# Three order edits at the two ends of a fused attention and MLP kernel: token transposes, the queries' PSUM bank, one addition of the drain

## The chip, the cores and the metric

The kernel runs on one core of one Trainium2 chip, in one launch. Its time is device time in microseconds of that core. The kernel before takes 1280.31 us (median of 3 runs, 1280.17 to 1280.67).

The core has engines with a queue of their own each: TensorE (PE in the profile; its weight loads are PEld), VectorE (DVE), ScalarE (ACT), GpSimd (POOL) and SyncE (SP, which here only issues transfers). Each engine executes its queue in order. They meet through semaphores. Matmuls write to PSUM, a memory of eight banks, from which VectorE and ScalarE read.

## The reference

Tokens are layer-normed once. Branch A is attention of 2048 tokens against a cache of 2048 keys and values with 32 heads of 128; branch B is an MLP with two layer norms; the output gates the one with the other.

```python
def _A_ref(x, k_cache, v_cache, wq, wo):
    q = (x @ wq).reshape(B, Sq, H, Dh).transpose(0, 2, 1, 3)
    scores = einsum("bhqd,bhkd->bhqk", q, k_cache) * (Dh ** -0.5)
    p = softmax(scores, axis=-1)
    o = einsum("bhqk,bhkd->bhqd", p, v_cache)
    return o.transpose(0, 2, 1, 3).reshape(B, Sq, H * Dh) @ wo

def _B_ref(x, w1, w2, w3, w4):
    h = gelu(layernorm(x) @ w1)
    hs = shifted(h) @ w2          # each quarter of h moved by 1 or 2 tokens
    x1 = x + hs
    return x1 + gelu(layernorm(x1) @ w3) @ w4

xn = layernorm(x)
s = _A_ref(xn, k_cache, v_cache, wq, wo)
g = silu(_B_ref(xn, w1, w2, w3, w4))
out = x + s * g
```

Everything is bfloat16 in memory, with 2048 tokens of 512 elements; the MLP is 1792 wide.

## The kernel before, in words

**Units and slots.** The attention is cut into 128 units (line 121): a unit is one head and one block of 512 tokens. Units run by groups of 4 heads, in a group by token block, in a block by head. So units 0 to 3 are heads 0 to 3 on tokens 0 to 511, unit 4 is head 0 on tokens 512 to 1023. A unit has 8 slots. In slot `p` of unit `u`, which is step `n = 8u + p` of the loop at line 695, these are written down in order:

- `s_slot`: two matmuls of 128 keys each against the 512 queries `qT` into the PSUM tile `ps_s` (two of them, two banks each), then ScalarE's exponential of both into `pT` (line 194).
- `pv_slot`: the two matmuls of the values for the slot five steps back (`LAG = 5`), into `ps_o`.
- In slots 0 and 1, `q_mm`: the queries of unit `u + 2` (four matmuls, `ps_q`), and in slot 2 their copy to `qT` by `q_copy`: VectorE's (line 180), but ScalarE's (line 178) for the last units, `u > QUIET + 1`, that is units 123 to 127 (`QUIET` is 121).
- In slot 3, `sums`: four narrow matmuls with a vector of ones give the row sums of unit `u - 1` (`ps_sum`); VectorE takes the reciprocal (line 233), a small transfer writes it to DRAM (`dr`, line 235), and in slot 4 a broadcast reads it back for all partitions (`rb`, line 250). In slot 2 of the next unit, `norm` (line 261) multiplies `ps_o` by it.
- In slots 4 to 6, `wo_mm` (`ps_wo`, the output projection of one tile of 128 tokens that is ready) and its addition to `s_acc` on VectorE (line 328).
- VectorE also adds up the exponentials (`acc`, lines 200 to 211), of which `sums` takes the row sums.
- Chunks of the MLP in slots 2, 3, 6 and 7, with their PSUM tile `ps_m`, until unit 120.

**The two shared PSUM banks.** The pool `psX` has one buffer for each of two tags. "xa" holds `ps_q`, `ps_wo` and `ps_sum`; "xm" holds the MLP's `ps_m`, and from unit 121 on also `ps_sum` (line 225). The next tile of a tag can be written only when the last has been read.

**Order.** `pin` keeps each engine's instructions in the order in which they are written down. Loads are put at steps of the loop by `at(n, ...)`, and run at the end of that step (line 759). SyncE's queue holds the K loads (transposing transfers, a quarter of a head's keys each, line 146), the V loads (half a head each, line 156), the token transposes (`ln1_turn`, line 370), `dr` and `rb`.

**The start.** Token tiles of 128 are normalised on VectorE with GpSimd's reciprocal roots (line 354) and then turned into `xnT`, the operand of the queries. Tiles 0 to 3 are turned on TensorE. Tiles 4 to 7 are turned by transfers after steps 5, 12, 13 and 14 (the third number of each triple in `tokens`, line 661). The queries of unit 4 (`HG`) are made in slots 6 and 7 of unit 2, steps 22 and 23, and need tiles 4 to 7. Lines 670 to 673 put the K pieces and V halves of heads 2 and 3 at their steps.

**The end.** `gate_sum` (lines 299 and 301) is put into units 122 and 124 in slot 4, for two of the last token tiles, on VectorE. In the drain (lines 788 to 807) the last four token tiles are scaled from PSUM by `last_scale` (line 305, VectorE) and added to `s_acc` by `last_out` (line 310), which also issues the output transfer (line 311).

Of the kernel before, what the change touches and what calls it, by code (L numbers as in the profile page):

```python
# [10 lines left out]
FP32 = mybir.dt.float32  # L11
# [6 lines left out]
def kernel(  # L18
# [16 lines left out]
    P = nc.NUM_PARTITIONS  # L35
# [15 lines left out]
    HG = 4 if H % 4 == 0 else (2 if H % 2 == 0 else 1)  # L51
# [13 lines left out]
    def pool(name, bufs=1, space=None, **kw):  # L65
        if space is not None:
            kw["space"] = space
        return tc.tile_pool(name=name, bufs=bufs, **kw)
# [35 lines left out]
    psX = ent(pool("psX", 1, PSUM))  # L104
# [8 lines left out]
    def mm(out, lhsT, rhs, start, stop):  # L113
        pin(nc.tensor.matmul(out=out, lhsT=lhsT, rhs=rhs, start=start, stop=stop))  # L114
# [8 lines left out]
    QUIET = NU - 7  # L123
# [3 lines left out]
    kTs, vBs, wqs, wos, oTs, st = {}, {}, {}, {}, {}, {}  # L127
    todo = defaultdict(list)

    def at(n, fn):  # L130
        todo[n].append(fn)
# [9 lines left out]
    def load_k(h, pieces):  # L141
        w = Sk // KSPLIT
        for i in pieces:
            if i == 0:
                kTs[h] = kp.tile([P, Sk], BF16, name="kT")
            pin(nc.sync.dma_start(
                out=kTs[h][:, i * w:(i + 1) * w],
                in_=A_k_cache[0, h, i * w:(i + 1) * w, :], transpose=True))

    def load_v(h, halves):  # L150
        v = A_v_cache[0, h].rearrange("(i p j) d -> p i j d", p=P, j=KJ)
        for i in halves:
            if i == 0:
                vBs[h] = vp.tile([P, KC, Dh], BF16, name="vb")
            ks = slice(i * KSPLIT // 2, (i + 1) * KSPLIT // 2)
            pin(nc.sync.dma_start(
                out=vBs[h].rearrange("p (i j) d -> p i j d", j=KJ)[:, ks], in_=v[:, ks]))
# [9 lines left out]
    def q_mm(u, dcs):  # L167
        g, qt, hh = units[u]
        if dcs[0] == 0:
            st[u] = dict(psq=psX.tile([P, 512], FP32, tag="xm" if u == HG else "xa", name="ps_q"))  # L170
        for dc in dcs:
            mm(st[u]["psq"][:], wqs[g * HG + hh][:, dc, :],
               xnT[:, dc, qt * 512:(qt + 1) * 512], dc == 0, dc == DC - 1)
# [129 lines left out]
    def last_scale(t, ps):  # L303
        gf, xf = tl[t]
        pin(nc.vector.scalar_tensor_tensor(
            out=gf[:], in0=ps, scalar=0.5, in1=gf[:], op0=ALU.mult, op1=ALU.mult))

    def last_out(t, eng):
        gf, xf = tl.pop(t)
        pin(eng.tensor_tensor(out=xf[:], in0=gf[:], in1=s_acc[:, t, :], op=ALU.add))  # L310
        pin(nc.sync.dma_start(out=out2d[t * P:(t + 1) * P, :], in_=xf[:]))
# [57 lines left out]
    def ln1_turn(t):  # L369
        pin(nc.sync.dma_start_transpose(out=xnT[:, :, t * P:(t + 1) * P], in_=xns.pop(t)[:]))  # L370
# [293 lines left out]
    for t, (stats, apply, turn) in enumerate(tokens, 4):  # L664
# [2 lines left out]
        at(stats, lambda t=t: ln1_stats(t))  # L667
        at(apply, lambda t=t: ln1_apply(t))
        at(turn, lambda t=t: ln1_turn(t))
    for n, h, piece in ((2, 2, 2), (4, 2, 3), (12, 3, 0), (15, 3, 1), (17, 3, 2), (20, 3, 3)):  # L670
        at(n, lambda h=h, piece=piece: load_k(h, (piece,)))
    for n, h, half in ((7, 2, 0), (13, 2, 1), (20, 3, 0), (21, 3, 1)):
        at(n, lambda h=h, half=half: load_v(h, (half,)))
    at(28, ph1_load)
    at(64, w2_load)
# [2 lines left out]
    for g in range(NG - 1):  # L678
        b = (g * QT + QT - 1) * HG
        for hh in range(HG):  # L680
            h = (g + 1) * HG + hh
# [13 lines left out]
    for n in range(NS):  # L695
        u, p = divmod(n, SPU)
# [4 lines left out]
        if u == 0 and p in (1, 3, 5):  # L701
            q_mm(1 + p // 2, range(DC))
        if u == 0 and p in (2, 4, 6):
            q_copy(p // 2)
        if u == HG - 2 and p in (6, 7):
            q_mm(HG, (2 * p - 12, 2 * p - 11))
        if u == HG - 2 and p == 7:
            q_copy(HG)
        if p in (0, 1) and HG - 1 <= u < NU - 2:
            q_mm(u + 2, (2 * p, 2 * p + 1))  # L710
# [90 lines left out]
        wo_part(dst[j], GL, ts[j], range(HG), False, True)  # L801
    for j in range(4):
        last_scale(ts[j], dst[j])
        if j < 2:
            last_out(ts[j], nc.gpsimd)
    for j in (2, 3):
        last_out(ts[j], nc.vector)
    ph.close()

# [29 lines left out]
```

## Time and profile before

| what | value |
|---|---|
| median of 3 runs | 1280.31 us |
| the profiled execution | 1279.53 us |
| its span, first to last instruction | 1277.8 us |
| granted TensorE clock | 0.999 of full |
| exponentials (line 194, ScalarE) | 1024 of 1.03 us |
| matmuls of 512 columns (line 114) | 0.38 us each, started 0.216 us apart |
| VectorE, busy from 1206.2 to 1215.4 us (9.2 us) | 8.32 us |
| VectorE, busy from 1215.4 to 1224.2 us (8.8 us) | 6.95 us |
| last addition of the drain ends | 1274.76 us |

A group's line names the line of the code, the engine, the operation, the output and inputs by the program's names, and how often it ran. In a timeline a line has the start in us from the span's start, the time it took (for several merged instructions, from the first start to the last end), and what it is; in brackets stands how long its engine was idle before it, and what ended that. A line of waits has the engine, what waited, what it waited for, and the sum, the count and the longest in us. An SPq line is the issuing of a transfer; its landing comes later, and the DMA view tells how much later.

### The profile page before, as it was taken

The numbers are of one execution on the slowest core, as the hardware profiler recorded it, in microseconds if no ns is written. First come the engines' busy times: TensorE is split into PE (matmuls) and PEld (weight loads), VectorE is DVE, ScalarE is ACT, GpSimd is POOL, SyncE is SP. The second block draws the span as 40 slices with busy tenths as digits, with TensorE's granted clock in tenths as the row PEclk, the third lists the DMA queues.
The fourth block names the chain that finished last, engine by engine and source line by source line (L and its number), as shares of the span: only waits on it lengthen the run. The fifth ranks groups of instructions, "written<-read, shape, count | busy, mean of one in ns | idle before, by whom it ended". The sixth has DMA issues, their size and how long they took to land.

```text
span 1277.8 us, 17233 instructions
## 1 busy us (share of the span) xinstructions
PE 1257.1 (98%) x6195; PEld 612.1 (48%) x6320; DVE 1019.2 (80%) x1407; ACT 1113.0 (87%) x1195; POOL 137.9 (11%) x241
## 2 busy tenths in 40 slices
PE   8999999999999999999999999999999999999998
PEld 5444444444444444444444444444444444444444
DVE  7888889898788877778887778887777888777886
ACT  7899998888999988899988889998888999888883
POOL 4430003323110010000001000000000000000110
PEclk9999999999999999999999999999999999999999
DMA  9644343455532564134443244523435133542532
GB/s 185 133 106 81 59 79 88 108 124 123 115 77 67 100 110 89 42 75 83 89 93 68 58 85 93 96 42 75 96 80 90 34 70 72 91 105 46 140 76 58
DMA packets 172950, 111.79 MB, mean 87 GB/s; under 512 B 124800, under 2 KB 149888, under 8 KB 172864
## 3 DMA queue, kind: packets, MB, share of 16 engines
q1 hardware_dynamic: 163904, 85.51, 34.3%
q0 software_dynamic: 8672, 24.91, 7.9%
q8 instruction: 49, 0.80, 0.3%
q14 instruction: 37, 0.30, 0.1%
q10 hardware_dynamic: 288, 0.26, 0.1%
HBM read 82.58 MB, written 7.60 MB: 71 GB/s over the span
## 4 chain that ended last, share of the span: by engine, by line
PE 87%; ACT 6%; DVE 4%; issue 1%; DMA 1%; POOL 0%; DVEq 0%; ACTq 0%
PE ps_s L114 31%; PE ps_o L114 30%; PE ps_m L114 9%; PE ps_wo L114 8%; PE ps_q L114 7%; ACT pT L194 4%; PE ps_sum L114 1%; ACT sq L425 1%; DVE acc L205 1%; ACT pre L455 1%; DVE bn L349 0%; DMA rb<-dr 0%; DMA xnT<-xn 0%; DVE acc L210 0%; DVE qT L180 0%
## 5 line engine op out<-in xcount | busy, mean ns | idle before, releaser
L194 ACT ACTIVATE pT<-ps_s 128x1024 bf16<-128x1024 f32 x1024 | 1012.0, 1031 | 141.0 <-PE ps_s L114 130.0
L114 PE MATMUL ps_s<-qT,kT 128*128 128x512 bf16 x2004 | 599.5, 379 | 4.1 <-ACT pT L194 1.0
L114 PE MATMUL ps_o<-pT,vb 128*128 128x512 bf16 x1997 | 597.6, 379 | 2.8
L205 DVE TENSOR_TENSOR acc<-acc,pT 128x2048 bf16<-128x2048 bf16 x254 | 309.8, 1220 | 65.5 <-ACT pT L194 60.8
L114 PEld LDWEIGHTS <-kT 128*128 128x128 bf16 x2048 | 226.8, 113 | 224.4 <-issue 18.6
L114 PEld LDWEIGHTS <-vb 128*128 128x128 bf16 x2048 | 199.8, 98 | 225.2
L200 DVE TENSOR_TENSOR acc<-pT 128x2048 bf16<-128x2048 bf16 x128 | 155.9, 1218 | 26.6 <-ACT pT L194 26.4
L114 PE MATMUL ps_q<-xnT,wq_h 128*128 128x512 bf16 (+1 forms) x519 | 150.7, 374 | 3.3 <-DMA xnT<-xn 2.0
L114 PE MATMUL ps_wo<-wo_h,oT 128*128 128x512 bf16 x456 | 136.3, 379 | 0.6
L328 DVE TENSOR_TENSOR s_acc<-ps_wo,s_acc 128x512 f32<-128x512 f32 x100 | 68.9, 689 | 73.9 <-PE ps_wo L114 71.0
L210 DVE TENSOR_TENSOR acc<-acc 128x1024 bf16<-128x1024 bf16 x127 | 87.9, 692 | 4.4
L261 DVE TENSOR_TENSOR oT<-ps_o,rb 128x512 bf16<-128x512 f32 x129 | 87.1, 676 | 4.1 <-DMA rb<-dr 4.0
L180 DVE CAST qT<-ps_q 128x512 bf16<-128x512 f32 x122 | 83.5, 685 | 4.8 <-PE ps_q L114 4.8
L114 PEld LDWEIGHTS <-wq_h 128*128 128x128 bf16 x524 | 50.6, 98 | 63.2 <-issue 3.6
L114 PEld LDWEIGHTS <-oT 128*128 128x128 bf16 x480 | 46.9, 98 | 57.7 <-issue 2.6
L114 PE MATMUL ps_m<-xn2T,w_sb 128*128 128x512 bf16 x222 | 66.1, 378 | 0.2
L114 PE MATMUL ps_m<-w_sb,h2T 128*128 128x512 bf16 x218 | 62.7, 379 | 0.2
L577 POOL DMA_DIRECT2D w_sb<-in_B_w_dram x28 | 21.1, 756 | 353.8 <-PE ps_m L114 328.6
L211 DVE TENSOR_TENSOR acc<-acc 128x512 bf16<-128x512 bf16 x127 | 54.0, 425 | 4.3
L233 DVE RECIPROCAL rc<-ps_sum 128x4 f32<-128x4 f32 x128 | 22.9, 179 | 40.9 <-PE ps_sum L114 40.0
L114 PEld LDWEIGHTS <-acc 128*128 128x128 bf16 x516 | 37.6, 115 | 29.6 <-issue 1.5
L609 POOL DMA_DIRECT2D g_d<-xr x16 | 8.8, 547 | 346.3 <-DVE xr L607 346.3
(74 smaller groups left out, 599.9 us busy)
## 6 DMA issues: line engine op xcount, KB each, us to landing
rb<-dr SPq DMA_DIRECT2D x128, 256.0 KB, 4.1
vb<-in_A_v_cache_dram SPq DMA_DIRECT2D x64, 256.0 KB, 4.5
w_sb<-in_B_w_dram POOLq DMA_DIRECT2D x28, 256.0 KB, 4.6
wo_h<-in_A_wo_dram SPq DMA_DIRECT2D x32, 128.0 KB, 3.9
wq_h<-in_A_wq_dram SPq DMA_DIRECT2D x28, 128.0 KB, 4.2
kT<-in_A_k_cache_dram SPq DMA_TRANSPOSE x128, 4.7
dr<-rc SPq DMA_DIRECT2D x128, 2.0 KB, 1.4
xr<-in_A_x_dram POOLq DMA_DIRECT2D x16, 128.0 KB, 3.5
```

The costliest lines, as they stand in the source:

```text
L114: pin(nc.tensor.matmul(out=out, lhsT=lhsT, rhs=rhs, start=start, stop=stop))
L180: pin(nc.vector.tensor_copy(out=qT[:], in_=st[u].pop("psq")[:]))
L194: pin(nc.scalar.activation(out=s["pT"][-1][:, jj:jj + 2, :], in_=sps[:], func=ACT.Exp, scale=SCALE))
L200: pin(nc.vector.tensor_tensor(out=s["acc"][:], in0=s["pT"][0][:], in1=s["pT"][1][:], op=ALU.add))
L205: pin(nc.vector.tensor_tensor(out=a[:], in0=a[:], in1=st[u]["pT"][i][:], op=ALU.add))
L210: pin(nc.vector.tensor_tensor(out=a[:, 0:2, :], in0=a[:, 0:2, :], in1=a[:, 2:4, :], op=ALU.add))
L211: pin(nc.vector.tensor_tensor(out=a[:, 0, :], in0=a[:, 0, :], in1=a[:, 1, :], op=ALU.add))
L233: pin(nc.vector.reciprocal(out=rc[:], in_=ps[:]))
L261: pin(nc.vector.tensor_tensor(out=oTs[(g, qt)][:, hh, c], in0=s["o"][:, c], in1=s["rb"][:, c], op=ALU.mult))
L328: pin(nc.vector.tensor_tensor(out=sa, in0=ps[:], in1=sa, op=ALU.add))
L425: pin(nc.scalar.activation(out=sq[:], in_=pre[:], func=ACT.Square, scale=GELU_A ** 0.5))
L577: pin(nc.gpsimd.dma_start(out=w[:], in_=w3_v[:, :, fc * P:(fc + 2) * P]))
```

## The change

Five lines differ. The K pieces 0 and 1 of head 3 move from steps 12 and 15 to steps 14 and 16; the second V half of head 2 moves from step 13 to step 15. The queries of units 123 to 127 get the tag "xm" in place of "xa". In the drain the addition of the second of the last four tiles moves from GpSimd to VectorE, behind all four scalings.

```diff
     def q_mm(u, dcs):
         g, qt, hh = units[u]
         if dcs[0] == 0:
-            st[u] = dict(psq=psX.tile([P, 512], FP32, tag="xm" if u == HG else "xa", name="ps_q"))
+            st[u] = dict(psq=psX.tile([P, 512], FP32, tag="xm" if u == HG or u > QUIET + 1 else "xa", name="ps_q"))
...
-    for n, h, piece in ((2, 2, 2), (4, 2, 3), (12, 3, 0), (15, 3, 1), (17, 3, 2), (20, 3, 3)):
+    for n, h, piece in ((2, 2, 2), (4, 2, 3), (14, 3, 0), (16, 3, 1), (17, 3, 2), (20, 3, 3)):
         at(n, lambda h=h, piece=piece: load_k(h, (piece,)))
-    for n, h, half in ((7, 2, 0), (13, 2, 1), (20, 3, 0), (21, 3, 1)):
+    for n, h, half in ((7, 2, 0), (15, 2, 1), (20, 3, 0), (21, 3, 1)):
         at(n, lambda h=h, half=half: load_v(h, (half,)))
...
     for j in range(4):
         last_scale(ts[j], dst[j])
-        if j < 2:
+        if j == 0:
             last_out(ts[j], nc.gpsimd)
-    for j in (2, 3):
+    for j in range(1, 4):
         last_out(ts[j], nc.vector)
```

On SyncE the queue goes from tile 5, K piece, tile 6, V half, tile 7 to tile 5, tile 6, tile 7, K piece, V half; what stands before and behind keeps its order. TensorE's order is the same as before; five of its row-sum matmuls get a wait on ScalarE. VectorE has one instruction more and GpSimd one less.

## The prediction

> **What bounds the kernel now.** I read the page first (engine shares, the chain that ended last), then the waits of TensorE, then the timeline around each of the three edits.
>
> ```profile
> PE 1257.1 (98%) x6195; PEld 612.1 (48%) x6320; DVE 1019.2 (80%) x1407; ACT 1113.0 (87%) x1195; POOL 137.9 (11%) x241
> ...
> PE 87%; ACT 6%; DVE 4%; issue 1%; DMA 1%; POOL 0%; DVEq 0%; ACTq 0%
> ```
>
> TensorE is busy nearly all the time and is 87% of the chain. So time can only come from the few places where TensorE waits, and an edit costs time only where it makes a new wait. The view of its waits has two that the change aims at:
>
> ```profile
> PE ps_q L114 <- DMA xnT<-xn: 2.0, 1, 2.0
> ...
> PE ps_q L114 <- DVE s_acc L328: 0.8, 2, 0.5
> ```
>
> **Edit 1, token transposes ahead of K and V (lines 670 and 672).** The timeline of SyncE's queue (start, time to issue, what):
>
> ```profile
> 25.00 1.19 SPq L370 DMA_TRANSPOSE xnT<-xn  x1
> 26.24 1.25 SPq L146 DMA_TRANSPOSE kT<-in_A_k_cache_dram  x1
> 27.59 1.21 SPq L370 DMA_TRANSPOSE xnT<-xn  x1
> 28.85 0.59 SPq L156 DMA_DIRECT2D vb<-in_A_v_cache_dram  x1
> 29.54 1.19 SPq L370 DMA_TRANSPOSE xnT<-xn  x1
> 30.77 2.56 SPq L146 DMA_TRANSPOSE kT<-in_A_k_cache_dram  x2
> 33.43 0.52 SPq L235 DMA_DIRECT2D dr<-rc  x1
> 35.18 0.32 SPq L250 DMA_DIRECT2D rb<-dr  x1
> 35.55 1.12 SPq L146 DMA_TRANSPOSE kT<-in_A_k_cache_dram  x1
> 36.73 1.08 SPq L156 DMA_DIRECT2D vb<-in_A_v_cache_dram  x2
> ```
>
> The rows at 25.00, 27.59 and 29.54 are token tiles 5, 6 and 7. The queries of unit 4 need all of them and start at 33.98. Matmuls start 0.216 us apart, so a pair takes 0.43; the pair before (31.43) was through at 31.86, and the wait is really 33.98 - 31.86 = 2.12 us. The change moves one K piece of head 3 (1.25 us of SyncE) and one V half of head 2 (0.59) behind tile 7, which goes out at 25.00 + 2 x 1.25 = 27.5 in place of 29.54 (its tokens are normalised by 26.5). The DMA view of short windows gives 3.5 us to landing for the transpose issued at 27.59, so tile 7 lands at about 31.0, ahead of 31.86: the wait goes.
>
> What is late next: the K piece, at 28.7 + 4.3 (its own time to landing) = 33.0, used at 35.71 - 2.12 = 33.6; the V half, at 30.0 + 4.5 = 34.5, used at 37.43 - 2.12 = 35.3. Both hold by less than a microsecond. Nothing else in the queue moves: seven issues of the same lengths end at about 33.4 as before, then SyncE waits for the small `dr` transfer (issued 33.43, the broadcast behind it at 35.18), and the V half of head 3 goes out at 36.73 and lands 4.5 later, at 41.2. Its first user is the ps_o pair that started at 41.80, with no wait then; TensorE would now reach it at 39.68. Landing to start was 33.85 to 33.98, 0.13, so it starts at 41.33: 1.65 of the 2.12 us are given back and 0.47 stay. Then at 57.39 TensorE waits 0.43 us for a VectorE copy whose chain starts at the landing of a broadcast (issued 44.01, used 48.41); that chain moves earlier by somewhere between nothing and 0.37 (VectorE's own gain at the broadcast of 35.18, which lands at 39.8, used now at 40.23). I take **-0.25 us**. Bounds: -2.12 if V came as soon as it is wanted (the shortest V landing of this stretch, 3.0, would nearly do it); +0.8 if SyncE's seven issues stretch by one long transpose (1.86 in place of 1.2, the row at 14.17) and V takes the longest landing of the stretch, 5.1: 36.73 + 0.66 + 5.1 + 0.13 - 41.80.
>
> **Edit 2, queries of units 123 to 127 in the MLP's bank (line 170).** The timeline of one late unit:
>
> ```profile
> 1208.58 1.02 ACT L194 ACTIVATE pT<-ps_s 128x1024 bf16<-128x1024 f32 x1 [0.33 <-PE ps_s L114]
> ...
> 1209.18 0.59 PE L114 MATMUL ps_o<-pT,vb 128*128 128x512 bf16 x2
> ...
> 1209.49 0.59 ACT L178 ACTIVATE qT<-ps_q 128x512 bf16<-128x512 f32 x1
> 1209.61 0.27 PE L114 MATMUL ps_sum<-ones_t,acc 128*128 128x1 bf16 x4
> ...
> 1214.66 0.68 DVE L328 TENSOR_TENSOR s_acc<-ps_wo,s_acc 128x512 f32<-128x512 f32 x1
> ...
> 1215.40 0.59 PE L114 MATMUL ps_q<-xnT,wq_h 128*128 128x512 bf16 x2 [0.51 <-DVE s_acc L328]
> ```
>
> Removed: the queries shared bank "xa" with ps_wo, so twice (1215.40 and 1233.41) they waited until VectorE, late by the gate sums, had added ps_wo. By the pitch both waits are 0.46 us (ready at 1214.94 and 1232.95): **-0.92**; the view's 0.81 is the other bound.
>
> Added: from unit 121 on the row sums (ps_sum) already lie in "xm", one buffer. Now the queries of unit u+2 fill that bank in slots 0 and 1 of unit u, ScalarE copies them out behind the exponential of slot 2, and the row sums of slot 3 must wait for that copy. In the rows: sums at 1209.61, copy from 1209.49 to 1210.09. With 0.06 for the signal (L328 ends at 1215.34, TensorE starts at 1215.40) the sums start at 1210.08 + 0.06 = 1210.14, 0.53 us late. All five copies of line 178 start 0.12 us before their sums, so it recurs in units 121 to 125: 5 x 0.53 = **+2.65** (5 x 0.48 without the signal, 5 x 0.6 with a slower restart). Queued behind the sums on TensorE are the scores of the next slot and all else; nothing covers it, since a unit without a wait takes 8.78 us (1215.40 to 1224.17) for 40 large matmuls of 0.216 and the sums, 8.77. ScalarE has 0.33 us of slack in front of the exponential, so the copy cannot come earlier, nor does lateness shrink it. VectorE's late additions no longer matter: its next reader, ps_wo of the next unit, comes half a unit later.
>
> The Trainium skill (PSUM — Partial Sum Buffer, section "PSUM bank collisions raise a hardware error") says to guard PSUM by the bank, not by the address, with semaphores. By that rule the sums could not start beside the copy even in another column of the bank; in the rows above they overlap because they are in two banks. It speaks against this edit and gives the same 2.65.
>
> Sum of edit 2: +1.73 (bounds +1.5 and +2.2).
>
> **Edit 3, one addition from GpSimd to VectorE (lines 804 to 807).**
>
> ```profile
> 1271.33 2.27 POOL L310 TENSOR_TENSOR xf<-gf,s_acc 128x512 bf16<-128x512 bf16 x2 [29.12 <-DVE gf L305]
> ...
> 1272.36 0.68 DVE L305 SCALAR_TENSOR_TENSOR gf<-ps_wo,gf 128x512 bf16<-128x512 f32 x1
> ...
> 1272.96 1.80 DVE L310 TENSOR_TENSOR xf<-gf,s_acc 128x512 bf16<-128x512 bf16 x2
> ```
>
> By line, VectorE's two additions take 1.20 and 0.68 us, GpSimd's 1.15 each. VectorE's slow one (1272.96 to 1274.16) overlaps GpSimd's second (to 1273.63); the fast one runs alone. With one GpSimd addition (over by 1272.48) I price three on VectorE as unhindered: starts 0.60 apart like the scalings of line 305, end 1272.96 + 2 x 0.60 + 0.68 = 1274.84 against 1274.76: **+0.08**. Bounds: -0.1 (starts 0.5 apart, nearer than any row here) and +1.1 if 1.20 is what any addition but the last costs (starts 1.12 apart).
>
> The Trainium skill (SBUF — State Buffer, section "Who interferes with whom") states that a VectorE instruction with two SBUF inputs contends with a GpSimd instruction that reads SBUF, and the loser is blocked. By it the 1.20 is contention and goes with the second GpSimd addition; the scaling at 1272.36, with one input in PSUM, ran beside GpSimd in 0.68, as the rule has it. That is why I give the +1.1 little.
>
> **The sum.** -0.25 + 1.73 + 0.08 = +1.56 us. The profiled execution took 1279.53 (span 1277.8 and 1.7 around it) and would take 1281.1. It was 0.78 below the median of the runs, 1280.31, so the forecast is 1281.9. A change of 0.2%, 2.56 us, is about what a measurement can tell; so my forecast is a loss inside that bound.
>
> **Rivals.**
> - A: the first wait is won whole. Needs the V half of head 3 by 39.7, that is 3.0 us after its issue. For it: V landed in 3.0 once. Against: the broadcast issued 1.5 us ahead of it takes 4.6 itself. -2.12 + 1.73 + 0.08: 1280.0, not slower.
> - B: the sums don't wait (the copy gets in front). For it: ScalarE idles 0.33. Against: the copy is behind an exponential that needs the very scores issued two pairs before. -0.25 - 0.92 + 0.08: 1279.2. With A too: 1277.4, faster.
> - C, slower: three additions in the drain at 1.12 apart. It decides if the first VectorE addition takes over 1 us with GpSimd idle. +1.12 in place of 0.08: 1282.9.
> - D, slower: the delayed V half of head 2 comes after 37.4 (7.3 us after issue; the longest landing in these 62 us is 7.0) and TensorE stands still there, a microsecond for each microsecond. For it: one more transpose lands ahead of it. Against: neighbouring transposes land some 0.5 us apart, and it was 4.5 us on the way. At 8.5 us, 1.2 on top of edits 2 and 3: 1283.3.
>
> **How the numbers follow.** Forecast 0.64, A 0.13, B 0.05 and with A 0.03, C 0.08, D 0.07. The range 1279.6 to 1283.2 leaves out B, A with B and the far side of D; the forecast's own is 1281.3 to 1282.6 (edit 1 from -0.47 to 0, edit 2 from 1.5 to 2.2). Faster by over 0.2% (below 1277.75): A with B, 0.04. Slower (above 1282.87): C, D and the upper edge of the forecast, 0.18. Within: 0.78.
>
> **What would show it.** Right: no wait near 32, a new one of 1.5 us for `vb` near 40; line 178 ahead of five waits of ps_sum of about 0.5 us near 1201, 1210, 1219, 1229, 1238; none of ps_q on L328; three additions of 0.68. Wrong: ps_sum starting beside line 178, no wait for `vb`, or an addition of 1.2 with GpSimd idle.

## The result, and the profile after

The changed kernel takes 1282.15 us (median of 22 runs, 1281.17 to 1283.42) against 1280.18 us for the kernel before (22 runs): a ratio of 1.0015 with a 95% interval of [1.0008, 1.0021], so it is slower, by 1.97 us. The forecast was 1281.9 us, 1.56 us more than before. The profiled execution took 1281.79 us, its span is 1280.0 us against 1277.8.

The page and the view of TensorE's waits of the changed kernel (engine, what waited, for what: sum in us, times, longest):

```profile
PE 1258.6 (98%) x6195; PEld 613.0 (48%) x6320; DVE 1019.6 (80%) x1408; ACT 1113.5 (87%) x1195; POOL 138.2 (11%) x240
...
PE 84%; ACT 7%; DVE 4%; DMA 2%; issue 1%; POOL 0%; SPq 0%; DVEq 0%; ACTq 0%
```

```profile
PE ps_sum L114 <- ACT qT L178: 1.8, 5, 0.4
PE ps_o L114 <- DMA vb<-in_A_v_cache_dram: 1.7, 1, 1.7
...
PE ps_sum L114 <- DVE qT L180: 0.9, 2, 0.7
```

The two waits that the change aimed at are no longer in the list: ps_q waits neither for `xnT` nor for line 328. In their place stand five waits of the row sums for ScalarE's copy, and one of the values' matmul for V. The wait of the row sums for VectorE's copy, which was 0.4 us at the longest, is 0.7.

The timeline at the start (SyncE's queue, and the TensorE pair that waits):

```profile
24.91 0.34 SPq L250 DMA_DIRECT2D rb<-dr  x1
25.30 3.83 SPq L370 DMA_TRANSPOSE xnT<-xn  x3
29.17 1.25 SPq L146 DMA_TRANSPOSE kT<-in_A_k_cache_dram  x1
30.48 0.57 SPq L156 DMA_DIRECT2D vb<-in_A_v_cache_dram  x1
31.10 2.57 SPq L146 DMA_TRANSPOSE kT<-in_A_k_cache_dram  x2
33.76 0.52 SPq L235 DMA_DIRECT2D dr<-rc  x1
35.41 0.32 SPq L250 DMA_DIRECT2D rb<-dr  x1
35.78 1.12 SPq L146 DMA_TRANSPOSE kT<-in_A_k_cache_dram  x1
36.95 1.08 SPq L156 DMA_DIRECT2D vb<-in_A_v_cache_dram  x2
...
41.92 0.61 PE L114 MATMUL ps_o<-pT,vb 128*128 128x512 bf16 x2 [1.74 <-DMA vb<-in_A_v_cache_dram]
```

The three token transposes go out in one row, and everything from the `dr` transfer on goes out when it did before (33.76 against 33.43, with this execution 0.34 us late from its first tokens on). So V of head 3 leaves SyncE at 36.95, and TensorE, which is now early, waits for it.

The timeline of the same late unit as before (what ScalarE and TensorE do around the row sums):

```profile
1209.43 1.02 ACT L194 ACTIVATE pT<-ps_s 128x1024 bf16<-128x1024 f32 x1 [0.33 <-PE ps_s L114]
...
1210.03 0.59 PE L114 MATMUL ps_o<-pT,vb 128*128 128x512 bf16 x2
...
1210.35 0.59 ACT L178 ACTIVATE qT<-ps_q 128x512 bf16<-128x512 f32 x1
...
1210.99 0.27 PE L114 MATMUL ps_sum<-ones_t,acc 128*128 128x1 bf16 x4 [0.36 <-ACT qT L178]
```

The pair at 1210.03 is through after 0.43, at 1210.46; the row sums start at 1210.99, 0.05 behind the end of the copy (1210.94). That is 0.53 us by the pitch; the bracket says 0.36 because the view counts a matmul as busy until its modelled end. All five waits are 0.53 us by the pitch. The row sums come 9.29 to 9.30 us apart, where a unit without a wait took 8.78 before, so a wait lengthens its unit by a little less, some 0.51 us.

The timeline of the drain of the changed kernel (VectorE's scalings and additions, GpSimd's addition):

```profile
1272.70 1.89 DVE L305 SCALAR_TENSOR_TENSOR gf<-ps_s,gf 128x512 bf16<-128x512 f32 x3 [0.37 <-PE ps_s L114]
...
1273.48 1.16 POOL L310 TENSOR_TENSOR xf<-gf,s_acc 128x512 bf16<-128x512 bf16 x1 [29.25 <-DVE gf L305]
...
1274.51 0.68 DVE L305 SCALAR_TENSOR_TENSOR gf<-ps_wo,gf 128x512 bf16<-128x512 f32 x1
...
1275.10 1.88 DVE L310 TENSOR_TENSOR xf<-gf,s_acc 128x512 bf16<-128x512 bf16 x3
```

Three additions take 1.88 us on VectorE where two took 1.80. From the first scaling to the end of the last addition it is 4.28 us, before 4.21.

Where the 2.2 us between the two spans come from, read at the same instructions of both timelines:

| instruction | before | after | later by |
|---|---|---|---|
| first token turned on TensorE | 7.06 | 7.40 | 0.34 |
| row sums that wait for VectorE's copy, unit 4 | 57.39 | 57.77 | 0.38 |
| a score pair late in the middle | 1093.12 | 1093.46 | 0.34 |
| row sums with the last of the five waits | 1236.86 | 1238.87 | 2.01 |
| first scaling of the drain | 1270.55 | 1272.70 | 2.15 |
| last addition ends | 1274.76 | 1276.98 | 2.22 |

The first 0.34 us is there before any edited instruction runs: the first token load took 2.99 us in this execution, 2.66 in that of before. Edit 1 brought nothing that lasts (0.38 against 0.34), edit 2 cost 1.67 us, the last broadcast, which no edit touches, took 3.6 us to land in place of 3.0 and cost 0.14, edit 3 cost 0.07.

### The profile page after: what moved, and what is told of

Read it like the earlier page. It is cut to its first block, busy times and chain, and to the rows that moved or that the text cites. A ratio compares the mean times of both kernels' runs of the same rounds, so it can differ in the third digit from the quotient of the medians.

```text
span 1280.0 us, 17233 instructions
## 1 busy us (share of the span) xinstructions
PE 1258.6 (98%) x6195; PEld 613.0 (48%) x6320; DVE 1019.6 (80%) x1408; ACT 1113.5 (87%) x1195; POOL 138.2 (11%) x240
## 4 chain that ended last, share of the span: by engine, by line
PE 84%; ACT 7%; DVE 4%; DMA 2%; issue 1%; POOL 0%; SPq 0%; DVEq 0%; ACTq 0%
PE ps_s L114 31%; PE ps_o L114 29%; PE ps_m L114 9%; PE ps_wo L114 8%; PE ps_q L114 7%; ACT pT L194 5%; DVE acc L205 1%; PE ps_sum L114 1%; ACT sq L425 1%; DMA rb<-dr 1%; ACT pre L455 1%; DMA dr<-rc 1%; DVE acc L210 0%; DVE oT L261 0%; POOL rs L119 0%
## 5 line engine op out<-in xcount | busy, mean ns | idle before, releaser
L233 DVE RECIPROCAL rc<-ps_sum 128x4 f32<-128x4 f32 x128 | 22.9, 179 | 42.9 <-PE ps_sum L114 41.9
```

What stands on the lines that cost most here:

```text
L233: pin(nc.vector.reciprocal(out=rc[:], in_=ps[:]))
```

## The experiments

Times are medians; the ratio is that of each kernel's runs to runs of the kernel before on the same chip. In the short diffs the lines with a minus are the kernel before, if nothing else is said.

### Edit 1 alone

```diff
-    for n, h, piece in (..., (12, 3, 0), (15, 3, 1), ...):
+    for n, h, piece in (..., (14, 3, 0), (16, 3, 1), ...):
-    for n, h, half in ((7, 2, 0), (13, 2, 1), ...):
+    for n, h, half in ((7, 2, 0), (15, 2, 1), ...):
```

> Edit 1 alone. My theory: the 2.1 us wait of the queries near 32 us goes, TensorE waits about 1.7 us for a V half of head 3 near 42 us and some 0.3 us more than before at the row sums near 57 us; what is left is between -0.3 and +0.1 us (about 1280.1). Rival 1, the loss of the whole change sits here: +1.5 us or more. Rival 2, the wait is won whole: -2.1 us.

Measured: 1280.62 us against 1280.26, ratio 1.0002 [0.9993, 1.0010]. In its profile the wait for the tokens is gone and TensorE waits 1.1 us for V, at 40.94, where the kernel before was at 41.80 with the same start: 0.86 us are won there. At the row sums of unit 4 it waits 0.8 us for VectorE (the kernel before 0.4) and is 0.55 us ahead (56.84 against 57.39). One profile cannot show a gain of that size, since executions differ as much: from the first token turned on TensorE to these row sums the profiles with the queue of before (the kernel before, edits 2 and 3 alone, and the fourth experiment) take 50.10 to 50.54 us, those with edit 1 (this one, the changed kernel and the copies on VectorE) 49.79, 50.37 and 50.95. Both rivals fall: edit 1 neither loses 1.5 us nor wins 2.1.

### Edit 2 alone

```diff
-        ... tag="xm" if u == HG else "xa", name="ps_q"))
+        ... tag="xm" if u == HG or u > QUIET + 1 else "xa", name="ps_q"))
```

> Edit 2 alone. My theory: five waits of the row sums on ScalarE's copy, 0.53 us each by the pitch, and the two waits of ps_q on VectorE's addition (0.46 each) gone: +2.65 - 0.92 = +1.73 us (about 1281.9). Rival 1, the waits are hidden in slack of TensorE: -0.9 to 0 us. Rival 2, the loss of the whole change is edit 1's: -0.9 us here.

Measured: 1282.15 us against 1280.26, ratio 1.0015 [1.0006, 1.0024], 1.9 us. Its waits show the same first line as the changed kernel's:

```profile
PE ps_sum L114 <- ACT qT L178: 1.8, 5, 0.4
```

From the score pair at 1093.74 to the row sums at 1239.15 it takes 145.41 us, the kernel before 143.74 (1093.12 to 1236.86): 1.67 us, as in the changed kernel. The waits are not hidden, and the whole loss of the change is in this edit.

### Edit 3 alone

```diff
-        if j < 2:
+        if j == 0:
             last_out(ts[j], nc.gpsimd)
-    for j in (2, 3):
+    for j in range(1, 4):
```

> Edit 3 alone. My theory: three additions of 0.68 us on VectorE, 0.6 us apart, ending 4.29 us after the first scaling starts, in place of 4.21: +0.08 us. Rival: any addition of this form but the last takes 1.2 us there, +1.1 us.

Measured: 1280.30 us against 1280.26, ratio 1.0001 [0.9992, 1.0010]. The three additions take 0.68 to 0.69 us each, 0.60 apart, and end 4.29 us after the first scaling starts. The 1.20 us of the kernel before went with GpSimd's second addition.

### Edit 2 with the row sums in the other bank

```diff
-        ... tag="xm" if u == HG else "xa", name="ps_q"))
+        ... tag="xm" if u == HG or u > QUIET + 1 else "xa", name="ps_q"))
-        ps = psX.tile([P, 4], FP32, tag="xa" if u + 1 < QUIET else "xm", name="ps_sum")
+        ps = psX.tile([P, 4], FP32, tag="xa", name="ps_sum")
```

> Edit 2 alone, and the row sums back in the bank xa in the last units too, so that neither the queries nor the row sums share a bank with what is read late. My theory: it is the shared bank that costs, so the five waits go and the two old ones stay away: -0.92 us against the kernel before (about 1279.3). Rival: the wait moves on to ps_wo, which now follows the row sums in their bank and waits for their reciprocal (ready 0.5 us ahead in the trace of before): 0 us.

Measured: 1279.41 us against 1280.26, 0.85 us less, ratio 0.9994 [0.9986, 1.0003]; by the interval alone the sign is not certain. The profile decides: from 1094 us to the drain the view names no wait of TensorE, neither on ScalarE's copy nor on line 328, and from 1093.43 to the row sums at 1236.44 it takes 143.01 us, 0.73 less than the kernel before. So it is the place of the row sums that turned edit 2 into a loss. What is short of 0.92 is the rival's wait, at one place:

```profile
1201.70 0.59 PE L114 MATMUL ps_o<-pT,vb 128*128 128x512 bf16 x2
...
1202.10 0.17 DVE L233 RECIPROCAL rc<-ps_sum 128x4 f32<-128x4 f32 x1
...
1202.33 0.59 PE L114 MATMUL ps_wo<-wo_h,oT 128*128 128x512 bf16 x2
```

The pair at 1201.70 is through at 1202.13, and the next one, of `ps_wo`, starts 0.20 us later, 0.06 behind the end of the reciprocal. The row sums come 8.96 us apart across this wait and 8.78 behind it. In the profile of the two gains together all of them come 8.78 apart.

### The copies on VectorE

The changed kernel, with one line of it changed:

```diff
-        if u > QUIET + 1:
+        if u > NU:
             pin(nc.scalar.activation(out=qT[:], in_=st[u].pop("psq")[:], func=ACT.Identity))
         else:
             pin(nc.vector.tensor_copy(out=qT[:], in_=st[u].pop("psq")[:]))
```

> The changed kernel with the copies of the last units' queries on VectorE in place of ScalarE. My theory: the row sums wait for the copy because it is queued behind ScalarE's exponential; VectorE is free earlier, so the waits go in the units without a gate sum (121, 123, 125), and in the other two VectorE has 8.8 + 0.7 us of work in a unit of 8.8 and is late by up to 0.7 us each: 1279.7 to 1280.7. Rival: sharing the bank costs the wait whoever copies: five waits of 0.5 us, 1282.

Measured: 1279.96 us against 1280.33 for the kernel before, ratio 0.9991 [0.9982, 1.0000]. With the bank shared as in the changed kernel, the row sums of the late units wait for nothing, also in the units with a gate sum; they come 8.76 to 8.78 us apart, and VectorE's copies end 0.12 to 0.43 us ahead of them. So sharing alone does not cost the wait. It costs it because the copy stands in ScalarE's queue behind an exponential. My fear for the two units with a gate sum was wrong.

### V ahead of the small transfer

Edit 1, and:

```diff
-    for n, h, half in (..., (20, 3, 0), (21, 3, 1)):
+    for n, h, half in (..., (18, 3, 0), (21, 3, 1)):
```

> Edit 1 alone, and the first V half of head 3 issued ahead of the small transfer dr of unit 1 in SyncE's queue, in place of behind its broadcast. My theory: two things are late together where the 2.1 us went, the V half and the PSUM tile that is freed by VectorE's multiplication with the broadcast; V now lands before 39, the broadcast 0.6 us later than before, so the same matmul (first values of unit 3) waits for VectorE until about 41.2 and nothing is gained: 0 to -0.3 us at the row sums near 57. Rival: the V half is the only thing late; TensorE gets there at 39.7 and the row sums come 1.6 us earlier than in the kernel before, unless they wait for VectorE.

Measured: 1281.68 us against 1280.33, ratio 1.0011 [1.0001, 1.0020]. The timeline of its SyncE queue and of the pair that waited for V:

```profile
33.63 0.58 SPq L156 DMA_DIRECT2D vb<-in_A_v_cache_dram  x1
34.31 0.41 SPq L235 DMA_DIRECT2D dr<-rc  x1
36.86 0.34 SPq L250 DMA_DIRECT2D rb<-dr  x1
...
42.27 0.59 PE L114 MATMUL ps_o<-pT,vb 128*128 128x512 bf16 x2 [1.98 <-DVE oT L261]
```

V is there in time, and the same pair waits for VectorE's multiplication, hence for the broadcast, as the theory had it: two transfers were late together. The time missed my expectation on the wrong side, by over 1 us. `dr` took 2.5 us to land behind V, where it took 1.7 with edit 1 alone, so the broadcast went out at 36.86 and landed at 41.5; and behind the wait came the half clock that the last section shows, worth 1.7 us.

### `dr` and the broadcast in another queue

Edit 1, and for unit 1 alone:

```diff
-        recip(s, ps)
+        recip(s, ps, nc.gpsimd if u == 1 else nc.sync)
...
-        pin(nc.sync.dma_start(out=s["dr"][:], in_=rc[:]))
+        pin(eng.dma_start(out=s["dr"][:], in_=rc[:]))
...
-        pin(nc.sync.dma_start(
-            out=st[u]["rb"][:], ...
+        eng = nc.gpsimd if u == 1 else nc.sync
+        pin(eng.dma_start(
+            out=st[u]["rb"][:], ...
```

> Edit 1 alone, and dr and its broadcast of unit 1 issued by GpSimd's queue in place of SyncE's. My theory: it is SyncE's wait for dr, behind the row of transposes, that made V late; dr can now go out at 29.7 in place of 33.4, V of head 3 at 34.6 in place of 36.7, both land before TensorE comes at 39.7, and neither wait is left near 40. The row sums near 57 come 0.5 to 2 us earlier than before (they may wait for VectorE), and so does the end: about 1279.3. Rival: the transfers are bound by the DMA engines, not by the queue; V and the broadcast land where they did, and TensorE waits 1 to 1.7 us near 41 as with edit 1 alone: 0 us.

Measured: 1278.51 us against 1280.33, ratio 0.9983 [0.9974, 0.9992]. The timelines of its GpSimd and SyncE queues:

```profile
30.43 0.55 POOL L235 DMA_DIRECT2D dr<-rc  x1 [3.58 <-DVE rc L233]
...
34.16 0.54 POOL L251 DMA_DIRECT2D rb<-dr  x1 [3.18 <-DMA dr<-rc]
```

```profile
30.98 3.83 SPq L146 DMA_TRANSPOSE kT<-in_A_k_cache_dram  x3
34.85 1.09 SPq L156 DMA_DIRECT2D vb<-in_A_v_cache_dram  x2
```

`dr` leaves 3 us earlier than before, SyncE no longer waits for it, and V goes out at 34.85; in the changed kernel, which has the same edit 1, it was 36.95. TensorE has no wait at all between 13.2 and 38.4 us, nor near 40, and is at the row sums of unit 4 at 55.34, 2.05 us ahead of the kernel before, a gain that lasts to the end (the spans are 2.2 us apart). The broadcast landed at 38.5 and V at 39.2, where it was 40.4 and 41.9 in the changed kernel: the transfers were bound by the queue. The edit also holds back GpSimd's next token load, from 34.26 to 35.59; whether that helped V was not tried by itself.

### That queue without edit 1

The kernel before, with the diff of the last experiment alone.

> The kernel before with dr and its broadcast of unit 1 issued by GpSimd's queue, K and V where they were. My theory: both steps are needed. Tile 7 still goes out behind the K piece and the V half, at about 29.5, and TensorE still waits some 2 us for it near 34; V of head 3 comes early and nobody is there to use it; only the row sums near 57 may wait up to 0.4 us less: -0.4 to 0 us. Rival: the gain of 1.8 us is the other queue's alone, and the order of K and V gives nothing: -1.8 us.

Measured: 1281.44 us against 1279.95, ratio 1.0007 [0.9998, 1.0016]: nothing gained, and possibly a loss, where I had expected a little. TensorE waits 2.7 us for the tokens in this profile (2.0 before), and as in the V experiment half clock follows. The rival falls: the other queue showed no gain without edit 1, and edit 1 none without the other queue.

### The two together

Edit 1 with the other queue, edit 2 with the row sums in "xa", the drain as before.

> Edit 1 with dr and its broadcast of unit 1 in GpSimd's queue, edit 2 with the row sums in xa, the drain as before. My theory: the two gains are at two ends and add up: -0.92 us and what the third of this set gives, about 1278.4. Rival: a gain at the start is taken back by a later wait on VectorE or ScalarE: 1279.4.

Measured: 1276.93 us against 1280.33, ratio 0.9975 [0.9964, 0.9985]: 3.4 us less than the kernel before, 5.2 less than the changed one by the medians of each. The view of TensorE's waits holds none for a transfer, none of ps_q, and none of the row sums for ScalarE:

```profile
PE ps_s L114 <- DVE ident L84: 1.4, 1, 1.4
PE ps_sum L114 <- DVE qT L180: 0.9, 2, 0.7
PE ps_s L114 <- ACT pT L194: 0.7, 2, 0.4
```

It beats both kernels. The gain is more than I had expected, but its interval, 1.9 to 4.6 us, holds the 2.7 us that the two gains measured by themselves add up to (0.85 and 1.82).

## Why the prediction was right

**Edit 2, the term that decides.** The five waits of 0.53 us are there to the hundredth, in the units that were named; the two old ones are gone. Forecast +1.73, shown by edit 2 alone +1.67 in the profile. It came out of two rows of the kernel before: a copy that ends 0.47 us behind the start of row sums that will have to wait for it, in units in which TensorE has no slack. That the wait needs both the shared bank and ScalarE's order is shown by the two experiments that take away one of them. Rival B falls.

**Edit 1.** That 1.65 of the 2.12 us would be given back at V of head 3 was right in kind, and the place was the right matmul. The sizes, by the pitch: the wait for V was 1.90 us in the changed kernel, where V took 4.9 us to land, and 1.27 in edit 1 alone, where it took 4.5 as forecast; the forecast was 1.65. Tile 7 took 3.9 us to land, not 3.5, and was still in time. With TensorE early, GpSimd's next token load goes out at 37.88 in place of 39.65 and travels beside the broadcast and V, which I did not count; but in edit 1 alone it goes out early too (37.53), so it does not explain the difference, and the cause of the longer landing stays open. What is left at the row sums of unit 4 was forecast as 0.25 us: it was -0.04 in the changed kernel and 0.55 in edit 1 alone, and neither the timed runs nor the spread of the profiles can tell it from nothing. Rival A falls. The condition that I named for it, V by 39.7, was too weak: in the V experiment V landed at 36.6 and the same pair waited for the broadcast instead. The other queue brings both early.

**Edit 3.** +0.08 was forecast, +0.07 and +0.08 were measured, by the contention that the Trainium skill (SBUF — State Buffer, section "Who interferes with whom") describes: with GpSimd's second addition gone, no addition on VectorE takes over 0.69 us. Rival C falls. Rival D did not occur: the V half of head 2 landed at 33.9.

**The sum.** 1.56 against 1.97 us measured; the forecast lies inside the interval of the ratio, [1.0 us, 2.7 us]. By the profile the sum of the three terms was 1.67 + 0.07 + 0.04 = 1.78. Of the 0.22 us above the forecast edit 1 makes 0.29 (0.04 against -0.25), edit 2 takes away 0.06 and edit 3 0.01; but a term of 0.3 us at the start is within the spread of the profiles there. The rest to 1.97 us is within the interval too. Two slips of the working change nothing: A with B has a chance of 0.03 in one place and 0.04 in another, and the forecast's own range begins at 1281.4, not 1281.3, by the terms given for it (-0.47 + 1.5 + 0.08).

## What to carry to other kernels

A wait that is removed at one place is worth only what the next late transfer leaves of it: list, for the work behind it, when each operand is issued and landed, before pricing the gain. In a queue that issues in order, one small dependent transfer at the wrong place (here `dr`) delays all loads behind it; putting that pair into another engine's queue gained 1.8 us together with the new order of the loads, while neither the new order alone nor the other queue alone showed a gain. When a tile is moved to another buffer, look for who else lives there, and at how late the last reader's engine gets to it.

## What the runs showed of the hardware that was not expected

A wait of some 2 us of TensorE cost more than itself in two of these profiles. In the V experiment the granted clock falls to a half behind the wait of 1.98 us (stretch, its length, busy time and count of PE, PEld, DVE, ACT, POOL, granted clock, DMA share, GB/s):

```profile
42.00:43.00 1.00, 0.73 (x4) 0.33 (x4) 1.00 (x4) 0.00 (x0) 0.00 (x0) 0.92 0.67 215
43.00:44.00 1.00, 1.00 (x4) 0.44 (x3) 1.00 (x3) 0.34 (x1) 0.00 (x0) 0.50 0.14 13
44.00:45.00 1.00, 1.00 (x4) 0.29 (x2) 0.96 (x4) 0.68 (x1) 0.02 (x1) 0.50 0.67 136
45.00:46.00 1.00, 1.00 (x4) 0.31 (x3) 0.99 (x1) 0.63 (x1) 1.00 (x1) 0.50 0.05 6
46.00:47.00 1.00, 1.00 (x6) 0.44 (x5) 0.58 (x1) 0.65 (x2) 0.92 (x3) 0.88 0.82 131
```

TensorE is busy all the time from 43 us on, but matmul pairs start 0.85 us apart in place of 0.43, for 3.41 us by the clock's own record: 1.7 us lost. The same happened for 3.41 us behind the 2.73 us wait of the experiment with the other queue alone. The waits of 1.96 us in the kernel before and of 1.74 us in the changed one passed without it in their profiles. By the clock's record the halving starts 37.55 us after the clock was released to full in the V experiment and 30.72 us after it in the other, which is 11 and 9 times 3.413 us. So steps of that length seem to count. If so, what matters is how much of one step a wait fills: by the pitch 2.14 us in the V experiment, but 1.99 us in the kernel before, whose wait began 0.13 us ahead of its step. That this decides is an inference from few profiles and was not tried. The Trainium skill (TensorE: Matmul & The Clock Gate, section "What's actually happening") gives a free-running window of 3.4 us after which an idle TensorE is halved; the length agrees with the 3.41 us here, but by the page a whole window has to be idle, and here 1.98 us of idle time was enough, so the measurement decides.

It bears on the times: of the runs of the V experiment 6 of 10 had a mean granted clock of 0.998 or less (median 1282.55 us), the other 4 had 1280.18; with the other queue alone it was 7 of 11 (1281.69) and 4 (1279.55); of the kernel with both gains none of 8. For the changed kernel it was 4 of 22, for the kernel before 14 of 78 in the same sets. The mark is rough: with edit 1 and the other queue, where the profile shows no wait of TensorE over 0.4 us from 13 us to the drain, it was 2 of 11, and these two were near the median (1278.72 and 1278.57 against 1278.51). So removing a wait of about 2 us probably also removes a chance of losing 1.7 more; that was not tried by itself.
